# Sampled rows of V by two indirect DMAs of GpSimd a tile, in place of six register-addressed DMAs of the sync engine

## The chip, the cores and the metric

The kernel runs on one core of one Trainium2 chip. A core has a matrix engine (TensorE, here PE, with its weight loads as PEld), a vector engine (VectorE, DVE), a scalar engine (ScalarE, ACT), a general engine (GpSimd, POOL) and a sync engine (SyncE, SP), which here only issues DMAs. Each engine works through its own instructions in order and waits on semaphores of the others. Sixteen DMA engines move the data. The metric is the device time of one execution in microseconds (us).

## The reference

Block-sparse attention over 4 batches, 8 heads, 768 positions of 64 values, and then a two-layer feed-forward network (FFN) over the 3072 tokens of 512 values. A query block of 32 positions sees its own block and both neighbours, the first and the last block, and three sampled blocks; the first and the last query block see everything.

```python
scores = scale * np.matmul(q, k.transpose(0, 1, 3, 2))
mask = np.abs(blk_i - blk_j) <= 1
mask = mask | (blk_i == 0) | (blk_j == 0) | (blk_i == n_blocks - 1) | (blk_j == n_blocks - 1)
for qb in range(n_blocks):
    for kb in sampled_blocks[qb]:
        mask[qb * 32:(qb + 1) * 32, kb * 32:(kb + 1) * 32] = True
attn = softmax(np.where(mask, scores, -1e9))
x = np.matmul(attn, v)                  # heads side by side: 3072 x 512
h = x @ w_in                            # 512 -> 2048
return np.maximum(0.01 * h, h) @ w_out  # 2048 -> 512
```

`sampled_blocks` is an input (24 x 3 block numbers), so the rows that a tile needs are known only on the chip.

## The kernel before

**Tiles.** A tile `T` is two query blocks (64 queries). Each batch has 12; tile 0 holds the first and the last block and sees all keys, the other 11 see 384 gathered keys: 12 slots of 32. In 4 batches that makes 44 gathered tiles. Before the change slots 0 to 3 are the window of four consecutive blocks, 4 and 5 the first and the last block, 6 to 11 the six sampled blocks (`sampled_of`, L569). Every value is split into a high and a low half in float16, so products are done in several matmuls.

**A tile's keys and values.** `gather_k` (L576) builds `kg`, the gathered K: a copy of the window on DVE (L582), the end blocks once a batch (L585), and then for each sampled block a register load of its offset on POOL (L590, from `offs`) and a copy on POOL (L591). `gather_v` (L605) builds `vg`, the gathered V: 128 partitions by 3 chunks, slot `s` in partitions 32·(s mod 4) of chunk s // 4. V's split rows lie in a DRAM scratch tensor `scr`, 2 KB a row. SP issues one DMA for the window (L611), two for the end blocks when the buffer is first used in a batch (L616), and for each of the six sampled blocks it loads the offset into a register (L619) and issues a DMA of 32 rows (L621). `kg` and `vg` have two buffers each, so a gather for tile T waits until PE is done with tile T-2.

**The rest of a tile.** Scores `s` on PE (L651, the first factor is the transposed q, `qs`, and its copy with swapped halves, `qxs`); row maxima with the mask on DVE (L658, `mx`); exponentials on ACT (L669); normalized high halves `pp` on ACT (L687) and low halves on DVE (L691); a DMA transpose of `pp` into `pt` issued by SP (L696); the product with `vg` on PE (L722, `av`). The output goes through ACT, DVE and POOL into `x` (L729 to L740). Q is prepared in halves of an item (four tiles): scaled, transposed by a DMA on SP (L535, `qs`) and copied with swapped halves (L537, L538). K is transposed once a batch in the same way (L512, `kt`).

**The FFN.** An item's 256 tokens go through in 8 chunks: first product `h` on PE (L757), leaky maximum on ACT and DVE (L764, L768, `ht`, one buffer), the high half of `g` on DVE (L773), the low half on POOL (L774), second product `o` on PE (L787, which needs both halves). The weights arrive as 64-bit values and are decoded on DVE and ACT (L310 to L316) and split (L371 to L376) during the first 200 us or so.

**What sets the order.** The program is written as one long list of steps, by tile and head pair, with the side work in between. A scheduler with a modelled timeline then sets each engine's order, so a step whose engine changes can move others on every engine. `in_order` (L558) adds order-only dependencies that keep the register-addressed instructions of one kind in sequence.

## Time and profile before

| | us |
|---|---|
| median of 3 runs | 904.76 |
| lowest and highest | 899.24, 905.93 |
| the profiled execution | 903.64 |
| its span, first to last instruction | 902.0 |
| DMA packets of SP's queue, share of 16 engines' span | 69.4% |
| mean granted clock of TensorE | 0.941 |

The profile is of one execution. A line such as `L691 DVE ...` gives the line of the program, the engine and the operation; the name ahead of the arrow is the tile that is written, the names behind it are read. Busy time counts an engine's own instructions, not what it issues: SP's register loads and DMA issues appear only in views of its queue (`SPq`). A wait is put down to the instruction that released the waiting one last. The granted clock is the share of full speed that the throttle gave TensorE. The busy digits of PE and DVE in 40 slices of 22.6 us show two stages: DVE-heavy at first, then PE-heavy.

```profile
PE   1324536688996988998997999889998999999998
...
DVE  4988889989876857757657656658676677655221
...
PEclk9999555899997999999998999999999999999999
```

### The profile page before, as it was taken

To read this page: it belongs to the slowest core of one execution; us is meant where nothing else is said; L and a number is where in the kernel's file an instruction comes from. 1 tells how busy PE (TensorE), PEld (TensorE's weight loads), DVE (VectorE), ACT (ScalarE), POOL (GpSimd) and SP (SyncE) were. 2 spreads that over 40 slices of the span, in tenths; PEclk is the share of its full clock that TensorE was granted. 3 is DMA by queue.
4 is the path that set the end of the run, shared out by engine and by line. 5 is a ranking of instruction groups with operands and counts; after the bars stand their busy time and mean duration, and the time that the engine had idled before them with its cause. 6 is when DMAs were issued, how large, how long until landed. Compare 5 with 4: busy or idle time off the path is not lost. (4 is left out here: it accounts for less than half of the span.)

```text
span 902.0 us, 21419 instructions
## 1 busy us (share of the span) xinstructions
PE 741.3 (82%) x7020; PEld 485.8 (54%) x7020; DVE 619.6 (69%) x1643; ACT 487.2 (54%) x1063; POOL 329.2 (37%) x469
## 2 busy tenths in 40 slices
PE   1324536688996988998997999889998999999998
PEld 0213234346564655665654665556665666656674
DVE  4988889989876857757657656658676677655221
ACT  4665765658554655556546545556455556544211
POOL 0143653724124334343423443334314354431221
PEclk9999555899997999999998999999999999999999
DMA  9994687778787697675776978766676857455100
GB/s 219 274 302 114 164 236 182 196 158 160 157 186 166 143 182 158 154 153 122 177 184 142 192 140 162 162 135 150 153 143 157 146 127 164 111 127 126 10 22 24
DMA packets 333294, 139.35 MB, mean 154 GB/s; under 512 B 296061, under 2 KB 308350, under 8 KB 333182
## 3 DMA queue, kind: packets, MB, share of 16 engines
q1 hardware_dynamic: 333182, 137.98, 69.4%
q8 instruction: 55, 0.90, 0.4%
q14 instruction: 57, 0.47, 0.2%
HBM read 65.57 MB, written 12.58 MB: 87 GB/s over the span
## 5 line engine op out<-in xcount | busy, mean ns | idle before, releaser
L757 PE MATMUL h<-x,W 128*128 128x256 f16 x2304 | 279.7, 278 | 1.1 <-DVE q_tot L140 0.8
L787 PE MATMUL o<-W,g 128*128 128x512 f16 x1152 | 275.1, 384 | 5.7 <-DVE g L773 3.3
L757 PEld LDWEIGHTS <-W 128*128 128x128 f16 x2304 | 226.2, 101 | 47.9 <-issue 8.3
L774 POOL TENSOR_TENSOR g<-ht,g 128x512 f16<-128x512 f32 x96 | 113.7, 1185 | 247.8 <-DVE g L773 173.7
L591 POOL COPY kg<-kt 128x256 f16 x264 | 124.0, 488 | 179.1 <-PE s L651 100.9
L669 ACT ACTIVATE p<-p,mx 128x384 f32<-128x384 f32 x208 | 126.2, 608 | 113.1 <-DVE mx L658 83.3
L691 DVE SCALAR_TENSOR_TENSOR pp<-p,r,pp 128x384 f16<-128x384 f32 x208 | 142.0, 713 | 56.5 <-ACT pp L687 55.9
L787 PEld LDWEIGHTS <-g 128*128 128x128 f16 x1152 | 107.9, 99 | 132.3 <-issue 16.7
L687 ACT ACTIVATE pp<-p,r 128x384 f16<-128x384 f32 x208 | 115.5, 607 | 63.6 <-DMA pt<-pp 23.7
L658 DVE CUSTOM_DVE_ANT_0 p<-s,em,nsc 128x384 f32<-128x384 f32 x176 | 102.4, 610 | 29.5 <-PE s L651 29.5
L768 DVE SCALAR_TENSOR_TENSOR ht<-h,gd,ht 128x512 f32<-128x512 f32 x80 | 59.7, 747 | 63.0 <-ACT ht L764 62.8
L722 PE MATMUL av<-pt,vg 128*64 128x128 f16 x2112 | 81.7, 228 | 19.3 <-DMA pt<-pp 12.2
L722 PEld LDWEIGHTS <-vg 128*64 128x64 f16 x2112 | 71.1, 114 | 42.0 <-issue 37.1
L764 ACT ACTIVATE ht<-h,gs 128x512 f32<-128x512 f32 x80 | 54.2, 677 | 68.1 <-PE h L757 53.8
L651 PE MATMUL s<-kg,qs_q 128*64 128x384 f16 x352 | 64.7, 365 | 31.5 <-DVE mx L658 24.8
L651 PEld LDWEIGHTS <-qs_q 128*64 128x64 f16 x416 | 27.6, 114 | 99.8 <-issue 64.7
L740 POOL TENSOR_TENSOR x<-xf,x 128x256 f16<-128x256 f32 x48 | 36.8, 766 | 101.9 <-ACT x L738 101.5
L651 PE MATMUL s<-kg,qxs_q 128*64 128x384 f16 x352 | 62.9, 356 | 9.7 <-DMA qxs_q<-qs_q 9.7
L677 DVE TENSOR_SCALAR sum<-sum 128x2 f32<-128x2 f32 x96 | 32.4, 337 | 37.4 <-ACT p L669 36.9
L773 DVE CAST g<-ht 128x512 f16<-128x512 f32 x96 | 42.0, 437 | 9.4 <-PE o L787 7.8
L651 PE MATMUL s<-kt,qs_q 128*64 128x384 f16 x64 | 12.8, 394 | 33.1 <-DVE mx L658 17.1
L669 ACT ACTIVATION_READ_ACCUMULATOR p<-p,mx 128x1 f32 x208 | 39.3, 189 | 0.0
(126 smaller groups left out, 728.9 us busy)
## 6 DMA issues: line engine op xcount, KB each, us to landing
vg<-scr SPq DMA_DIRECT2D x280, 64.0 KB, 1.8
vg<-scr SPq DMA_DIRECT2D x44, 256.0 KB, 3.7
v<-in_v_dram SPq DMA_DIRECT2D x32, 192.0 KB, 5.1
qxs_q<-qs_q SPq DMA_DIRECT2D x48, 128.0 KB, 2.6
scr<-v SPq DMA_DIRECT2D x16, 384.0 KB, 5.1
W<-in_moe_w_in_dram SPq DMA_DIRECT2D x5, 1024.0 KB, 6.1
rq<-in_q_dram SPq DMA_DIRECT2D x20, 256.0 KB, 3.7
out_dram<-ob SPq DMA_DIRECT2D x20, 256.0 KB, 2.8
```

Of the source, the lines that this page charges most:

```text
L591: nc.gpsimd.tensor_copy(out=kg[:, :, slot * BLOCK:(slot + 1) * BLOCK], in_=kt[:, :, bass.ds(off, BLOCK)])
L651: nc.tensor.matmul(o, a, k, start=(n == 0), stop=(n == 1)))
L658: nc.vector.tensor_tensor_reduce(out=u.p[i], in0=u.sp[i], in1=kgs[u.b, u.T][1] if u.T else zero.to_broadcast([P, KEYS]), scale=u.nsc, scal ...
L669: nc.scalar.activation(u.p[i], u.p[i], AF.Exp, scale=-1.0, bias=u.mx[:, :1], accum_out=u.pair.sum[:, u.pi, i:i + 1])
L687: nc.scalar.activation(pp[:, 0, :], p, AF.Copy, scale=u.r)
L691: nc.vector.scalar_tensor_tensor(out=pp[:, 1, :], in0=p, scalar=u.r, in1=pp[:, 0, :], op0=ALU.mult, op1=ALU.subtract)
L722: nc.tensor.matmul(o, a, m, start=(c == 0 and l == 0), stop=(c == n - 1 and l == 1)))
L757: nc.tensor.matmul(c.ph[:, i], w, x, start=(d == 0 and m == 0), stop=(d == NP - 1 and m == 2)))
L764: nc.scalar.activation(c.t, c.ph, AF.Copy, scale=scale[1])
L768: nc.vector.scalar_tensor_tensor(out=c.t, in0=c.ph, scalar=scale[0], in1=c.t, op0=ALU.mult, op1=ALU.max)
L774: nc.gpsimd.tensor_tensor(out=c.g[:, 1], in0=c.t, in1=c.g[:, 0], op=ALU.subtract)
L787: nc.tensor.matmul(o, a, w, start=(c.first and i == 0 and m == 0), stop=(c.last and i == 1 and m == 2)))
```

## The change

The six sampled blocks of a tile are no longer fetched by SP. A table `rows` (128 partitions x 2 chunks x 11 tiles) holds, for each partition, the row of V that belongs there: block number times 32 plus the lane within the block. It is filled once, at the start: six DMAs bring each sampled block number to 32 partitions, POOL writes the partition numbers into `lane`, and DVE combines them. `gather_v` then issues two indirect DMAs on POOL's queue, each with one column of `rows` as its list of row numbers: one for chunk 1 (128 rows) and one for chunk 2 (64 rows). For that the sampled blocks must fill whole chunks from their start, so the slots are reordered: the window keeps 0 to 3, the sampled blocks take 4 to 9, the end blocks 10 and 11. The mask, the copies into `kg` and the places in `vg` follow.

```diff
     def load_constants():
...
+        nc.vector.memset(rows, 0)
+        for s_ in range(2 * NR):
+            a, r = s_ // NR, s_ % NR
+            nc.sync.dma_start(
+                out=rows[s_ % 4 * BLOCK:(s_ % 4 + 1) * BLOCK, s_ // 4, :],
+                in_=sampled.bitcast(I32)[1 + a:NB - 2 + a:2, 2 * r].unsqueeze(0).to_broadcast([BLOCK, NT - 1]))
     def build_masks():
...
+        nc.gpsimd.iota(lane, pattern=[[0, 1]], base=0, channel_multiplier=1)
+        nc.vector.tensor_scalar(out=lane, in0=lane, scalar1=BLOCK - 1, scalar2=None, op0=ALU.bitwise_and)
+        flat_rows = rows.rearrange("p c t -> p (c t)")
+        nc.vector.scalar_tensor_tensor(
+            out=flat_rows, in0=flat_rows, scalar=5, in1=lane.to_broadcast([P, 2 * (NT - 1)]),
+            op0=ALU.logical_shift_left, op1=ALU.bitwise_or)
...
-            out=mask[:, :, 6:], in0=pm.rearrange("p t a r -> p t (a r)"), scalar1=-1.0, scalar2=-NEG,
+            out=mask[:, :, 4:10], in0=pm.rearrange("p t a r -> p t (a r)"), scalar1=-1.0, scalar2=-NEG,
             op0=ALU.add, op1=ALU.mult)
-        nc.vector.memset(mask[:, :, :6], 0.0)
+        nc.vector.memset(mask[:, :, :4], 0.0)
+        nc.vector.memset(mask[:, :, 10:], 0.0)
...
-        return [(6 + a * NR + r, (2 * T - 1 + a) * NR + r) for a in range(2) for r in range(NR)]
+        return [(4 + a * NR + r, (2 * T - 1 + a) * NR + r) for a in range(2) for r in range(NR)]
...
         nc.sync.dma_start(out=vg[:, 0, :], in_=scr[b][t0:t0 + P, :])
         if vends.get(n) != b:
             vends[n] = b
-            for slot, a in ((4, 0), (5, S - BLOCK)):
-                ps, c = place(slot)
-                nc.sync.dma_start(out=vg[ps, c, :], in_=scr[b][a:a + BLOCK, :])
-        for slot, i in sampled_of(T):
-            begin = len(nc.cur_bb.bb.instructions)
-            off = nc.sync.value_load(offs[:1, i:i + 1], min_val=0, max_val=S - BLOCK)
-            ps, c = place(slot)
-            nc.sync.dma_start(out=vg[ps, c, :], in_=scr[b][bass.ds(off, BLOCK), :])
-            in_order("v", begin)
+            for i, at in enumerate((0, S - BLOCK)):
+                nc.sync.dma_start(
+                    out=vg[Q2 + i * BLOCK:Q2 + (i + 1) * BLOCK, 2, :], in_=scr[b][at:at + BLOCK, :])
+        for c, n_ in ((1, P), (2, Q2)):
+            nc.gpsimd.indirect_dma_start(
+                out=vg[:n_, c, :], out_offset=None, in_=scr[b][:, :],
+                in_offset=bass.IndirectOffsetOnAxis(ap=rows[:n_, c - 1, T - 1:T], axis=0))
```

The scheduler's order follows. Line numbers of the changed kernel are 9 to 15 higher than before (L632 is the indirect DMA, L535 becomes L550, L696 becomes L708, L774 becomes L786). First SP, in the last item of the last batch, where the second half of Q is transposed (`qs_q3_2_1`). Before:

```order
L619 TENSOR_LOAD offs_89
L619 ISA x2
L621 ISA
L621 DMA vg1_96<-scr_3_12237 32x1024
L619 TENSOR_LOAD offs_89
L619 ISA x2
L621 ISA
L621 DMA vg1_96<-scr_3_12237 32x1024
L535 DMA_TRANSPOSE qs_q3_2_1_15871<-qa_q3_2_1_15455 128x8x128
L696 DMA_TRANSPOSE pt_3_2_0_3_15928<-pp_3_2_0_2_15743 128x12x128
L537 DMA qxs_q3_2_1_15873<-qs_q3_2_1_15871 64x1024
```

SP at the same place in the changed kernel:

```order
L708 DMA_TRANSPOSE pt_3_2_0_1_13376<-pp_3_2_0_0_13268 128x12x128
L708 DMA_TRANSPOSE pt_3_2_0_3_13505<-pp_3_2_0_2_13378 128x12x128
L625 DMA vg1_98<-scr_3_10394 128x1024
L708 DMA_TRANSPOSE pt_3_2_1_1_13607<-pp_3_2_1_0_13507 128x12x128
L550 DMA_TRANSPOSE qs_q3_2_1_13448<-qa_q3_2_1_13148 128x8x128
L552 DMA qxs_q3_2_1_13450<-qs_q3_2_1_13448 64x1024
```

The sampled gathers ahead of the transposes are gone; the transpose of q moved behind a transpose of the next tile's probabilities, which it used to precede. Second POOL, in batch 1, at the low halves `g_1_1_4` and `g_1_1_6` of two FFN chunks. Before:

```order
L596 CAST em_2_2_9181<-mask_90 128x384
L774 TENSOR_TENSOR g_1_1_4_8259<-ht_1_1_4_8256,g_1_1_4_8259 128x512
L590 TENSOR_LOAD offs_89
L590 ISA x2
L590 TENSOR_LOAD offs_89
L590 ISA x2
L740 TENSOR_TENSOR x_1_2_8169<-xf_1_2_1_2_8440,x_1_2_8169 128x4x64
L774 TENSOR_TENSOR g_1_1_6_8403<-ht_1_1_6_8400,g_1_1_6_8403 128x512
```

POOL at the same place in the changed kernel:

```order
L611 CAST em_2_2_7802<-mask_92 128x384
L786 TENSOR_TENSOR g_1_1_4_7054<-ht_1_1_4_7051,g_1_1_4_7054 128x512
L632 DMA vg1_98<-scr_1_3411,rows_90 128x1024
L605 TENSOR_LOAD offs_89
L605 ISA x2
L632 DMA vg1_98<-scr_1_3411,rows_90 64x1024
L605 TENSOR_LOAD offs_89
L605 ISA x2
L752 TENSOR_TENSOR x_1_2_6964<-xf_1_2_1_2_7177,x_1_2_6964 128x4x64
L786 TENSOR_TENSOR g_1_1_6_7140<-ht_1_1_6_7137,g_1_1_6_7140 128x512
```

A pair of indirect DMAs now stands between two low halves of g. Of the 44 pairs, 6 stand directly ahead of such an instruction and 8 with one instruction between. Third DVE, at the start, where the mask is made from the block numbers. Before:

```order
L532 SCALAR_TENSOR_TENSOR qa_q0_0_0_134<-rq_0_0_0_99,q0_0_0_s_143,qa_q0_0_0_134 128x8x64
L218 TENSOR_SCALAR offs_89<-tmps_88 1x72
L222 CAST sf_168<-tmps_88 24x3
L227 TENSOR_SCALAR tmps_88<-iota_87,sf_168 24x24 x3
L228 TENSOR_TENSOR hit_171<-tmps_88,allow_86 24x24
L311 TENSOR_SCALAR W_91<-W_91 128x1024
```

DVE at the same place in the changed kernel:

```order
L547 SCALAR_TENSOR_TENSOR qa_q0_0_0_143<-rq_0_0_0_101,q0_0_0_s_152,qa_q0_0_0_143 128x8x64
L226 TENSOR_SCALAR offs_89<-tmps_88 1x72
L236 CAST sf_180<-tmps_88 24x3
L232 SCALAR_TENSOR_TENSOR rows_90<-rows_90,lane_91 128x22
L241 TENSOR_SCALAR tmps_88<-iota_87,sf_180 24x24 x3
L242 TENSOR_TENSOR hit_183<-tmps_88,allow_86 24x24
```

The instruction that completes `rows` now stands between the cast to `sf` and the first comparison, ahead of the first decoding of the weights (L311 before).

More of the change, by code (lines that the diff above doesn't have):

```diff
@@ L207, in tile_block_sparse_attention_ffn @@
     offs = cst.tile([1, NB * NR], I32, name="offs")
+    rows = cst.tile([P, 2, NT - 1], I32, name="rows")
+    lane = cst.tile([P, 1], I32, name="lane")
     mask = cst.tile([P, NT - 1, SLOTS], F32, name="mask")
@@ L252, in build_masks @@
             nc.vector.memset(mask[b, :, 0:1], NEG)
-            nc.vector.memset(mask[a, 0:1, 4:5], NEG)
-            nc.vector.memset(mask[b, NT - 2:NT - 1, 5:6], NEG)
+            nc.vector.memset(mask[a, 0:1, 10:11], NEG)
+            nc.vector.memset(mask[b, NT - 2:NT - 1, 11:12], NEG)
     WI = 512
@@ L585, in gather_k @@
             nc.vector.tensor_copy(
-                out=kg[:, :, P:P + Q2].rearrange("p h (n l) -> p h n l", l=BLOCK),
+                out=kg[:, :, KEYS - Q2:].rearrange("p h (n l) -> p h n l", l=BLOCK),
                 in_=kt.rearrange("p h (n l) -> p h n l", l=BLOCK)[:, :, 0:NB:NB - 1, :])
@@ L609, in gather_v @@
         t0 = (T - 1) * Q2
-        place = lambda slot: (slice(slot % 4 * BLOCK, (slot % 4 + 1) * BLOCK), slot // 4)
         nc.sync.dma_start(out=vg[:, 0, :], in_=scr[b][t0:t0 + P, :])
```

## The prediction

> **What bounds the kernel now.** I read the header of the page first, then the busy time of each engine in four stretches, then the waits of TensorE (PE) in the two long ones.
>
> ```profile
> span 902.0 us, 21419 instructions
> PE 741.3 (82%) x7020; PEld 485.8 (54%) x7020; DVE 619.6 (69%) x1643; ACT 487.2 (54%) x1063; POOL 329.2 (37%) x469
> ...
> 0.00:67.50 67.50, 16.33 (x86) 10.44 (x86) 48.65 (x144) 38.57 (x68) 14.03 (x21) 1.00 1.12 265
> 67.50:225.00 157.50, 95.58 (x997) 65.40 (x998) 141.57 (x351) 101.68 (x203) 72.86 (x88) 0.78 0.74 173
> 225.00:860.00 635.00, 591.28 (x5686) 385.24 (x5684) 419.92 (x1134) 340.70 (x785) 233.10 (x352) 0.97 0.69 147
> 860.00:902.00 42.00, 38.08 (x256) 24.71 (x253) 9.42 (x16) 6.21 (x10) 9.25 (x8) 0.99 0.04 13
> ```
>
> The columns of the stretches are PE, weight loads, DVE, ACT, POOL, then the granted clock, the share of the DMA engines and GB/s. From 225 to 860 us PE is busy 591.3 of 635 us: it is the bound, and only 43.7 us of idle time can be won there. From 67.5 to 225 us DVE is busy 141.6 of 157.5 us (it decodes the weights beside the attention), so DVE is the bound there and at most 15.9 us can be won. The last 42 us are FFN matmuls that the change does not touch. SP has no busy time in such a table; what it is worth shows only in who waits for its DMAs. First PE's waits from 67.5 to 225 us, then from 225 to 860 us (total, times, longest):
>
> ```profile
> PE av L722 <- DMA pt<-pp: 12.7, 6, 4.7
> ...
> PE s L651 <- DMA qxs_q<-qs_q: 3.7, 2, 2.8
> PE s L651 <- DMA qs_q<-qa_q: 3.2, 1, 3.2
> ```
>
> ```profile
> PE s L651 <- DVE mx L658: 12.5, 6, 3.8
> PE av L722 <- DMA pt<-pp: 7.2, 4, 3.9
> PE s L651 <- DMA kt<-k_k: 6.9, 1, 6.9
> PE s L651 <- DMA qxs_q<-qs_q: 6.0, 4, 2.4
> ...
> PE s L651 <- DMA qs_q<-qa_q: 3.3, 2, 2.2
> ```
>
> All three DMAs named (pt, qs, qxs) are issued by SP, in order, between the blocks of V's gather. In neither list does PE wait for vg itself by a visible amount: the gathered rows arrive early enough today.
>
> **Part 1: what leaves SP.** One sampled block costs SP these instructions (min/median/max in ns):
>
> ```profile
> L619 SPq TENSOR_LOAD <-offs x264: 262/276/1097, 25.4 to 828.8; - x132
> L619 SPq FUSED_REGOPS  x264: 152/155/187, 25.9 to 829.1; - x132
> ...
> L621 SPq FUSED_REGOPS  x264: 37/37/52, 67.8 to 829.4; - x132
> L621 SPq MOVE vg<-scr x264: 29/29/38, 67.9 to 829.5; - x132
> L621 SPq DMA_DIRECT2D vg<-scr x264: 315/317/1605, 68.0 to 829.6; - x132
> ```
>
> 276 + 155 + 37 + 29 + 317 = 814 ns, times 264 blocks: 215 us of SP's time goes, about 4.9 us a tile. Almost all of it lies beside PE's work. Where it does not, it looks like this (SP's rows, then PE's):
>
> ```profile
> 789.12 6.28 SPq L621 DMA_DIRECT2D vg<-scr  x6
> 795.51 1.27 SPq L535 DMA_TRANSPOSE qs_q<-qa_q  x1
> ...
> 798.93 0.73 PE L651 MATMUL s<-kg,qs_q 128*64 128x384 f16 x4 [2.16 <-DMA qs_q<-qa_q]
> ```
>
> Six gathers hold SP for 6.28 us, the transpose of q goes out behind them, and PE stands 2.16 us. So what can come back from 225 us on is pt 7.2 + qxs 6.0 + qs 3.3 = 16.5 us; the 6.9 us for kt is one wait at a change of batch that hangs on the preparation of K, and I leave it out. The other end is 0: a transpose also has a landing time of its own, and in the new order the transposes are placed anew (in the rows of SP that the change section shows, qs now stands behind a pt that waits for the softmax). Half of the waits is as near to one end as to the other, and the one gap that I followed was caused by the gather, so I take **-8 us**, bounds -16.5 and 0. From 67.5 to 225 us PE waits 12.7 + 3.7 + 3.2 = 19.6 us for the same DMAs, but DVE is the bound and its whole idle time is 15.9 us; a PE that starts earlier helps only where DVE then waits less. I take a quarter of the 15.9, **-4 us**, bounds -15.9 and 0. What is late next where such a wait goes: the PSUM banks that DVE must empty (mx, 12.5 us).
>
> The plain load of a tile's window (L611) and the two end blocks stay on SP; SP's waits for a free vg stay with them. The order of the slots changes only which columns of kg, the mask and vg are written: same shapes, so 0. One small mask memset becomes two, at the very start, where DVE idles until the first sums of K: 0.
>
> **Part 2: the new index table at the start.** Six DMAs of 32 x 11 single words fill `rows`, in SP's queue ahead of the first transposes of K and q, and a DVE instruction that needs all six stands in DVE's order right behind the cast to sf. SP's and DVE's rows there, and what the DMA queues did from 5 to 30 us:
>
> ```profile
> 11.16 0.36 SPq L215 DMA_DIRECT2D tmps<-in_sampled_blocks_dram  x1
> 11.64 1.59 SPq L512 DMA_TRANSPOSE kt<-W  x1
> ...
> 15.73 0.16 DVE L222 CAST sf<-tmps 24x3 f32<-24x3 int32 x1 [0.51 <-DMA tmps<-in_sampled_blocks_dram]
> 15.93 0.51 DVE L227 TENSOR_SCALAR tmps<-iota,sf 24x24 f32<-24x24 f32 x3
> ...
> DMA packets 16061, 6.58 MB, mean 263 GB/s; under 512 B 15317, under 2 KB 15318, under 8 KB 16060
> ...
> q1 hardware_dynamic: 16060, 6.58, 119.7%
> ```
>
> Issuing: 6 x 0.36 = 2.2 us. Moving: 6 x 352 = 2112 packets of 4 bytes; a packet there took 1.197 x 16 x 25 us / 16060 = 29.8 ns of one engine, so 2112 x 29.8 ns / 16 = 3.9 us. Together 6.1 us by which kt, qs and DVE's instruction come later. DVE waits at 15.73 us already and is busy almost without a break after 22 us, so most of the delay runs through the DVE-bound stage; some is swallowed by the waits of the first 30 us. I take **+4 us**, bounds 0 and +6.1; a gain is excluded, since only a wait is added. The iota on POOL and the small `lane` instruction stand ahead of DVE's first sums, which wait for the loads of K: 0, hidden by these.
>
> **Part 3: what comes to POOL.** 88 indirect DMAs, two a tile, 128 and 64 rows. No row of before shows one. The nearest rows are POOL's own instructions that write 128 partitions:
>
> ```profile
> L774 POOL TENSOR_TENSOR g<-ht,g 128x512 f16<-128x512 f32 x96 | 113.7, 1185 | 247.8 <-DVE g L773 173.7 <-DVE sum L677 34.2 <-DVE r L678 9.5
> L591 POOL COPY kg<-kt 128x256 f16 x264 | 124.0, 488 | 179.1 <-PE s L651 100.9 <-issue 36.4 <-DMA kt<-W 18.1
> ...
> L374 POOL TENSOR_TENSOR W<-W 128x1024 f16<-128x1024 f32 x12 | 28.6, 2391 | 2.9 <-ACT W L373 2.2 <-POOL kg L591 0.5 <-ACT x L738 0.3
> ```
>
> Bounds 0.49 and 2.39 us each; I take 1.185 us, the middle row, for want of one that is nearer: 88 x 1.185 = 104 us more on POOL, from 329 to 433 of 902. POOL is no bound, but it works in order, and the low half of g (L774) that PE's second FFN product needs is in that order. How much room g has (POOL's rows, then PE's):
>
> ```profile
> 445.76 1.37 POOL L774 TENSOR_TENSOR g<-ht,g 128x512 f16<-128x512 f32 x1 [5.34 <-DVE g L773]
> ...
> 453.31 1.16 POOL L774 TENSOR_TENSOR g<-ht,g 128x512 f16<-128x512 f32 x1 [0.62 <-DVE sum L677]
> ...
> 458.30 1.16 POOL L774 TENSOR_TENSOR g<-ht,g 128x512 f16<-128x512 f32 x1 [1.36 <-DVE g L773]
> ...
> 447.19 1.90 PE L787 MATMUL o<-W,g 128*128 128x512 f16 x8 [0.22 <-POOL g L774]
> ...
> 458.23 1.89 PE L787 MATMUL o<-W,g 128*128 128x512 f16 x8
> ...
> 461.81 2.76 PE L787 MATMUL o<-W,g 128*128 128x512 f16 x12
> ```
>
> The three g end at 447.13, 454.47 and 459.46 us and are used at 447.19, 458.23 and 461.81: room of 0, 3.8 and 2.4 us, about 2.0 in the mean. In the new order of POOL 6 of the 44 pairs stand right ahead of a g and 8 more with one instruction between. A pair of 2.4 us is then 0.4 us longer than the room: 14 x 0.4 = **+5 us**. At 0.49 us it fits (0); at 2.39 us it is 14 x (4.8 - 2.0) = +39 us. A gain is excluded, POOL only gets work. The copies of kg have a tile's time of room and cost 0 while that holds. The DMA also waits on POOL, for PE to be done with the vg buffer two tiles before (SP did that until now), and behind it wait g, x and kg. I price that wait at 0 because in POOL's new order the pair mostly stands behind a g or x that itself waits for later work than that PE product.
>
> The Trainium skill, page "DMA: Bandwidth & Descriptors", section "Latency and other measured facts", puts the emission on GpSimd's cores at about 1 us; by it a pair is about 2.0 us, an estimate that just fits the room and makes this term 0 and the sum about 5 us lower. No run here has shown such a DMA yet.
>
> **The sum.** The profiled execution took 903.6 us, 1.6 of it around the span; the median of the runs shown is 904.8 (899.2 to 905.9), so I add 1.1. 903.6 - 8 - 4 + 4 + 5 = 900.6, and with the 1.1 about **902 us**: no change that a measurement tells (about 1%, 9 us, is what one can tell).
>
> **Rivals.** *SP's waits all go (faster).* For it: the gap at 798.93 us, and that such blocks, 4.9 us a tile, stand in all 44 tiles. Against: PE finds other work for most of that time already. It gives the full -16.5, half of DVE's idle time (-8), +4 for the table, POOL hidden: 904.8 - 20.5 = **884 us**.
>
> *POOL delays g (slower).* One mechanism: a pair ahead of g in POOL's order takes longer than g's room. It decides from about 1.6 us a DMA on, where 14 x (3.2 - 2.0) = 17 us: 904.8 - 12 + 4 + 17 = 914. At 1.8 us it is 14 x 1.6 = 22, less 12, plus 4: 904.8 + 14 = **919 us**; at 2.39 us 936 us. For it: the room of 0 at 447.19, and that ACT already waits for POOL:
>
> ```profile
>   ACT ht L764: 15.5, 8
> ...
>   PE o L787: 0.6, 2
> ```
>
> These are waits for POOL's g (total, times). Against: PE's own share of them is 0.6 us, and POOL is idle for 63% of the span.
>
> *Copies of DVE hold POOL's DMAs up (slower).* DVE casts g 96 times:
>
> ```profile
> L773 DVE CAST g<-ht 128x512 f16<-128x512 f32 x96 | 42.0, 437 | 9.4 <-PE o L787 7.8
> ```
>
> If each DMA waited for one such cast, a pair would be 0.87 us longer: 14 x (0.4 + 0.87) = 18 instead of 5, and the time 902 + 13 = **915 us**. Against: these casts are busy for under 5% of the span. The Trainium skill, page "SBUF — State Buffer", section "SBUF: two separate sides", warns of just this: while DVE runs such a copy GpSimd cannot write its DMA descriptors, and it advises the sync queue instead. The trace can bear on it only through POOL's copies of kg, whose mean of 488 ns leaves little room for such holds.
>
> *The transfer was hidden anyway.* Nothing on either queue matters and only the table counts: 904.8 + 4 = 909 us, within 1%.
>
> **Chances.** Forecast and hidden transfer, both within 1%: 0.42. SP's waits go: 0.30, all of it faster. POOL delays g: 0.22; held by DVE: 0.06; both slower. So faster 0.30, within 1% 0.42, slower 0.28. Range: below, all gains at their ends and no cost give 904.8 - 16.5 - 15.9 = 872; I cut at 882, which holds the first rival's 884. Above, 936 is the far end; 924 holds 919 and leaves about a tenth out on either side. The forecast's own range is 896 to 909.
>
> **What would show it.** Right: SP's rows without L619, vg rows on POOL of 1.0 to 1.5 us each; PE's waits for pt, qs and qxs after 225 us at about 8 us instead of 16.5; PE's wait for POOL's g up by some 5 us; DVE's first mask instruction (before at 15.93 us) some 6 us later; the 67.5 to 225 us stage ending about where it did. Wrong: DMA rows on POOL of over 1.6 us; a new wait of PE for vg, which I priced at 0; waits of POOL for PE ahead of its DMAs with g behind them; or a granted clock in the second stretch that is far from 0.78, which would move the time for a reason that I do not price.

## The result and the profile after

| | before | after |
|---|---|---|
| median of 4 runs, us | 904.42 | 917.0 |
| lowest and highest, us | 899.24, 905.93 | 915.16, 918.1 |
| profiled execution and its span, us | 903.64, 902.0 | 916.05, 914.1 |
| mean granted clock of TensorE | 0.941 | 0.936 |

The changed kernel is slower: ratio 1.0145, 95% interval 1.0111 to 1.0179, which is 13 us. Below, the gain or loss of a kernel is its ratio less one, times 904.4 us.

The stretches of the changed kernel (us, then the busy time of PE, weight loads, DVE, ACT and POOL, the granted clock, the share of the DMA engines, GB/s):

```profile
0.00:67.50 67.50, 15.43 (x76) 9.11 (x76) 41.76 (x139) 35.54 (x61) 12.87 (x22) 1.00 0.94 237
67.50:225.00 157.50, 98.70 (x988) 68.78 (x990) 147.99 (x348) 100.76 (x204) 92.33 (x106) 0.74 0.83 189
225.00:860.00 635.00, 589.83 (x5598) 381.46 (x5599) 437.21 (x1143) 339.64 (x785) 302.35 (x420) 0.97 0.73 145
860.00:914.00 54.00, 49.43 (x364) 31.91 (x362) 10.28 (x18) 9.05 (x14) 11.06 (x10) 0.98 0.06 20
```

From 225 to 860 us PE is no less idle than before (589.8 us of work against 591.3), although SP has lost six DMAs and six register loads a tile. Over the whole span PE is idle just as long as before, 160.7 us (902.0 less 741.3 us of work, 914.1 less 753.4). By the profile, then, the 12 us that the span has grown are longer times of the same 7020 matmuls (their ends are partly modelled). The granted clock is lower from 67.5 to 225 us, 0.74 against 0.78, which is one of the signs that the prediction named; but it is 0.75 there in `registers_fixed_rows` below too, which takes as long as the kernel before. POOL has 302 us instead of 233. DVE's timeline at the start shows what the table does:

```profile
14.99 0.15 DVE L236 CAST sf<-tmps 24x3 f32<-24x3 int32 x1 [0.65 <-DMA tmps<-in_sampled_blocks_dram]
22.48 0.18 DVE L232 SCALAR_TENSOR_TENSOR rows<-rows,lane 128x22 int32<-128x22 int32 x1 [7.33 <-DMA rows<-in_sampled_blocks_dram]
22.58 0.51 DVE L241 TENSOR_SCALAR tmps<-iota,sf 24x24 f32<-24x24 f32 x3
```

DVE stands 7.33 us for the six DMAs of single words; its first mask instruction starts at 22.58 us instead of 15.93. The indirect DMAs on POOL, and what POOL waited for ahead of them (us, times):

```profile
L632 POOL DMA_INDIRECT vg<-scr,rows x88: 899/998/1801, 68.5 to 836.9; - x88
its engine sat idle before it (us, times) until:
  PE av L734: 74.8, 23
```

An issue takes 1.0 us in the median. But ahead of 23 of them POOL stands, 74.8 us in all, until PE is done with vg, and everything behind it in POOL's order stands with it. PE's waits from 225 to 860 us for the transposes that SP issues have not fallen:

```profile
PE av L734 <- DMA pt<-pp: 10.1, 7, 4.3
PE s L663 <- DMA qxs_q<-qs_q: 9.3, 6, 4.5
...
PE s L663 <- DMA qs_q<-qa_q: 2.9, 3, 2.0
```

That is 22.3 us; it was 16.5. What stands ahead of these transposes shows in SP's own waits, which the prediction did not look at. First those of the kernel before, then those of the changed one (total, times, longest):

```profile
SPq L816 <- ACT ob L805: 66.0, 6, 40.4
SPq L696 <- PE av L722: 14.7, 11, 1.7
...
SPq L696 <- DVE pp L691: 9.5, 3, 8.0
SPq L611 <- PE av L722: 7.7, 6, 2.0
```

```profile
SPq L708 <- DVE pp L703: 96.9, 38, 10.6
SPq L625 <- PE av L734: 82.0, 25, 7.9
```

The 66.0 us for `ob` are stores of the output, 64.1 of them after 825 us. While attention ran, SP waited little before: the waits that its view lists from 225 to 825 us add up to 110 us, against 380 in the changed kernel. It reached the window's load (L611) so late that the buffer was nearly always free already. Now it waits, and in its new order a transpose of probabilities stands 38 times until DVE has written pp, with qs, qxs and the loads queued behind.

### The profile page after: what moved, and what is told of

It reads as the page before. It is cut to its first block, busy times and chain, and to the rows that moved or that the text cites. A ratio compares the mean times of both kernels' runs of the same rounds, so it can differ in the third digit from the quotient of the medians.

```text
span 914.1 us, 19932 instructions
## 1 busy us (share of the span) xinstructions
PE 753.4 (82%) x7020; PEld 491.3 (54%) x7020; DVE 637.2 (70%) x1647; ACT 485.0 (53%) x1063; POOL 418.6 (46%) x558
## 5 line engine op out<-in xcount | busy, mean ns | idle before, releaser
L799 PE MATMUL o<-W,g 128*128 128x512 f16 x1152 | 278.9, 386 | 9.9 <-DVE g L785 5.5
L786 POOL TENSOR_TENSOR g<-ht,g 128x512 f16<-128x512 f32 x96 | 115.8, 1206 | 206.3 <-DVE g L785 158.7
L703 DVE SCALAR_TENSOR_TENSOR pp<-p,r,pp 128x384 f16<-128x384 f32 x208 | 154.4, 772 | 32.4 <-ACT pp L699 31.4
L632 POOL DMA_INDIRECT vg<-scr,rows x88 | 94.0, 1068 | 94.3 <-PE av L734 74.8
L734 PE MATMUL av<-pt,vg 128*64 128x128 f16 x2112 | 87.6, 234 | 25.4 <-DMA pt<-pp 17.8
L734 PEld LDWEIGHTS <-vg 128*64 128x64 f16 x2112 | 74.2, 119 | 51.3 <-issue 47.0
L785 DVE CAST g<-ht 128x512 f16<-128x512 f32 x96 | 44.3, 462 | 11.6 <-PE o L799 10.1
L689 DVE TENSOR_SCALAR sum<-sum 128x2 f32<-128x2 f32 x96 | 27.7, 288 | 23.1 <-ACT p L681 22.3
L538 ACT ACTIVATE qa_q<-rq 128x512 f16<-128x512 f32 x25 | 15.7, 627 | 48.7 <-DMA rq<-in_q_dram 48.7
```

The source lines that it names most:

```text
L632: nc.gpsimd.indirect_dma_start(out=vg[:n_, c, :], out_offset=None, in_=scr[b][:, :], in_offset=bass.IndirectOffsetOnAxis(ap=rows[:n_, c - ...
L703: nc.vector.scalar_tensor_tensor(out=pp[:, 1, :], in0=p, scalar=u.r, in1=pp[:, 0, :], op0=ALU.mult, op1=ALU.subtract)
L734: nc.tensor.matmul(o, a, m, start=(c == 0 and l == 0), stop=(c == n - 1 and l == 1)))
L786: nc.gpsimd.tensor_tensor(out=c.g[:, 1], in0=c.t, in1=c.g[:, 0], op=ALU.subtract)
L799: nc.tensor.matmul(o, a, w, start=(c.first and i == 0 and m == 0), stop=(c.last and i == 1 and m == 2)))
```

## The experiments

### The table at the start

Theory A: the delay of the start runs through to the end. Theory B: the loss is POOL's. Kernel `table_only` adds the table (`load_constants` and `build_masks` as in the change) to the kernel before, used by nobody:

```diff
+    rows = cst.tile([P, 2, NT - 1], I32, name="rows")
+    lane = cst.tile([P, 1], I32, name="lane")
```

> The kernel before with the row table of the change added at the start (six DMAs of single words, the lane numbers, the combining DVE instruction) and used by nobody; V's rows still come by SP's register-addressed DMAs, and every engine keeps the order of before. Theory A (the table delays the start, and the delay runs through to the end): DVE stands 7.33 us at the combining instruction in the changed kernel, so about 904.4 + 7 = 911 us, ratio 1.007. Theory B (the loss is POOL's: its waits for PE and its 94 us of DMA issues): the start is swallowed, 904 to 906 us.

Measured: 910.15 us, ratio 1.0062 (1.0033 to 1.009), +5.6 us. `table_whole_words` is the changed kernel with other words in the table:

```diff
-                in_=sampled.bitcast(I32)[1 + a:NB - 2 + a:2, 2 * r].unsqueeze(0).to_broadcast([BLOCK, NT - 1]))
+                in_=sampled.bitcast(I32).rearrange("(o a) b -> o (a b)", o=1)[:, 6 * s_:6 * s_ + NT - 1].to_broadcast([BLOCK, NT - 1]))
```

> The changed kernel with the same six DMAs of the table, each of which reads 11 neighbouring words instead of 11 words that lie 48 bytes apart: 192 packets instead of 2112, the order of every engine but for this unchanged. The row numbers in the table are then others (still rows of V), so the sampled rows of V are not the reference's. Theory A: the wait of 7.33 us falls to 2 or 3 us and the time by 4 to 5, from 917 to about 912 us; DVE's first mask instruction 4 to 5 us earlier than 22.6. Theory B: no change, 917.

Measured: 910.52 us, ratio 1.0087 (1.0054 to 1.0119). DVE's wait fell as expected:

```profile
17.72 0.18 DVE L232 SCALAR_TENSOR_TENSOR rows<-rows,lane 128x22 int32<-128x22 int32 x1 [2.15 <-DMA rows<-in_sampled_blocks_dram]
```

5.2 us less of wait (the instruction starts 4.8 us earlier), 5.2 us less of time. So theory A holds for 5 to 6 of the 13 us. `table_from_row` keeps the table and drops its DMAs:

```diff
-    row = tmps[:1, 6:6 + 2 * NB * NR].bitcast(I32)
+    row = tmps[:, 6:6 + 2 * NB * NR].bitcast(I32)
...
+            nc.vector.scalar_tensor_tensor(
+                out=rows[ps, s_ // 4, :],
+                in0=row[ps, :].rearrange("p (n r l) -> p n r l", r=NR, l=2)[:, 1 + a:NB - 2 + a:2, r, 0],
+                scalar=5, in1=lane[ps, :].to_broadcast([BLOCK, NT - 1]),
+                op0=ALU.logical_shift_left, op1=ALU.bitwise_or)
```

> The changed kernel with the table built without DMAs of its own: the one DMA that brings the block numbers to partition 0 now brings them to all 128 partitions (576 bytes each), and six small DVE instructions shift, add the lane and place them. Everything is computed. The scheduler's order differs somewhat from the changed kernel's. Theory A: the whole 7 us of the start come back, less six DVE instructions of about 0.1 us: 917 - 6.5 = 910 to 911 us, ratio 1.007. Theory B: 917, ratio 1.014. If the rest of the loss comes from the new order rather than from POOL, the time may miss both by a few us.

Measured: 917.39 us, ratio 1.0177 (1.0134 to 1.022): a miss. In the first 67.5 us PE does 17.52 us of work instead of 15.43, so the start came back, and it was lost again from 225 us on, in an order of the scheduler that differs from the changed kernel's. A different order can thus be worth some 8 us by itself (1.0177 here against 1.0087 for `table_whole_words`, whose table costs no less); where it mattered, I chose edits that keep the order.

### What SP's gather had cost

`plain_on_sp` has neither table nor POOL's DMAs:

```diff
-            nc.gpsimd.indirect_dma_start(
-                out=vg[:n_, c, :], out_offset=None, in_=scr[b][:, :],
-                in_offset=bass.IndirectOffsetOnAxis(ap=rows[:n_, c - 1, T - 1:T], axis=0))
+            nc.sync.dma_start(out=vg[:n_, c, :], in_=scr[b][c * P:c * P + n_, :])
```

> The slots of the change, but the two DMAs of a tile (128 and 64 rows) are plain DMAs on SP that read fixed rows of V, with no table and no DMA on POOL: the sampled rows of V are not the reference's. It shows what freeing SP of the register loads and four of six DMAs is worth by itself. My forecast's relief of 12 us: 892 us, ratio 0.987. If the relief is worth nothing and POOL is what costs (theory B): 904. If SP's relief is worth nothing and the new order itself costs what theory A leaves open (917 - 7 - 904 = 5 to 6 us): 910.

Measured: 855.27 us, ratio 0.9473 (0.9441 to 0.9506). None of the three: freeing SP is worth 48 us, four times my forecast. The scheduler gave every engine a new order for it, so this is the relief together with that order. PE's waits from 225 to 860 us are then:

```profile
PE s L647 <- DMA qxs_q<-qs_q: 8.7, 6, 2.5
PE s L647 <- DVE mx L654: 5.5, 6, 1.6
...
PE k_sum L126 <- ACT k_k L495: 0.4, 1, 0.4
```

The waits for pt, qs and kt are no longer listed, those for mx have fallen from 12.5 us, and those for `k_k` from 5.0, where the kernel before had this line:

```profile
PE k_sum L126 <- ACT k_k L494: 5.0, 4, 2.3
```

`six_plain_on_sp` has six DMAs of 32 rows again, without register loads:

```diff
-            off = nc.sync.value_load(offs[:1, i:i + 1], min_val=0, max_val=S - BLOCK)
...
-            nc.sync.dma_start(out=vg[ps, c, :], in_=scr[b][bass.ds(off, BLOCK), :])
+            nc.sync.dma_start(out=vg[ps, c, :], in_=scr[b][slot * BLOCK:(slot + 1) * BLOCK, :])
```

> The kernel before in slots and engines, with six DMAs of 32 rows a tile on SP, but at fixed rows and so without the register loads (0.50 us of SP each of a block's 0.81): the sampled rows of V are not the reference's. If the register loads are what SP's gather costs the kernel before: close to plain_on_sp, 855 to 865 us. If it is the number of DMAs: 885 to 904 us.

Measured: 853.61 us, ratio 0.9439 (0.9401 to 0.9476). The number of DMAs costs nothing that shows (the order of every engine differs here too). Its SP waits for a free vg ahead of the window's load, as a queue with time to spare does, and from 225 us on PE gets its full clock:

```profile
SPq L611 <- PE av L719: 74.7, 20, 5.5
```

```profile
225.00:860.00 635.00, 606.65 (x5872) 400.40 (x5870) 425.40 (x1137) 345.91 (x790) 241.98 (x359) 1.00 0.70 145
```

`loads_fixed_rows` puts the loads back and does not use them; `registers_fixed_rows` also uses them, with fixed numbers in the registers. Both keep the order of PE, ACT and POOL of the kernel before. The second against the kernel before:

```diff
+        nc.gpsimd.iota(offv, pattern=[[BLOCK, 2 * NR]], base=P, channel_multiplier=0)
...
-            off = nc.sync.value_load(offs[:1, i:i + 1], min_val=0, max_val=S - BLOCK)
+            off = nc.sync.value_load(offv[:1, slot - 6:slot - 5], min_val=0, max_val=S - BLOCK)
```

> six_plain_on_sp (853.6 us) with the register loads put back on SP, one ahead of each of the six DMAs, but the DMAs still read fixed rows and do not use the registers, so the sampled rows of V are not the reference's. The order of PE, ACT and POOL is exactly that of the kernel before. If what the kernel before pays is SP's time for the loads (its queue is issuing for nearly all of the time from 225 to 825 us): about as before, 898 to 906 us. If it pays for the scattered rows or the register addressing of the DMAs: 853 to 865 us.

> The kernel before with every instruction and the order of every engine kept (one small iota on POOL added at the start), only that SP loads its six registers from a table of six fixed offsets: each tile then fetches the same 192 rows of its batch, which are not the reference's sampled rows. loads_fixed_rows, where the DMAs did not use the registers, took 881 us, the kernel before 903. If the 22 us between them are the register addressing of the DMAs: 903 us. If they are the scattered rows: 881 us.

Measured: 881.09 us, ratio 0.9752 (0.9727 to 0.9776), and 902.26 us, ratio 0.9989 (0.9963 to 1.0016). So the scattered rows cost nothing, and the register addressing 21 us, with the order kept. The loads cost 28 us against `six_plain_on_sp`, where the order of every engine differs as well, so these 28 are loads and order together. A load takes 276 + 155 ns of SP. The addressing takes only 37 + 29 ns, and the DMA itself 317 instead of 306 ns:

```profile
L621 SPq DMA_DIRECT2D vg<-scr x264: 302/306/1664, 67.9 to 808.2; - x132
```

264 x 431 ns = 114 us of SP cost 28 us, and the last 264 x 77 ns = 20 us cost 21. I read this as a queue that is full: the first work put on it is hidden, the last is paid one for one. That is not shown, and full cannot mean that SP never stands: its listed waits from 225 to 825 us add up to 139 us in `loads_fixed_rows` and 110 us in the kernel before (276 in `six_plain_on_sp`). `less_on_sp` moves V's loads, K's from the second batch on and the stores of the output to ACT, and was to test the reading from another side:

```diff
-            nc.sync.dma_start(out=t[:, :, h, :], in_=v[b, 2 * hp + h].rearrange("(c p) d -> p c d", p=P))
+            nc.scalar.dma_start(out=t[:, :, h, :], in_=v[b, 2 * hp + h].rearrange("(c p) d -> p c d", p=P))
...
-                nc.sync.dma_start(out=out[r0:r0 + P, :], in_=ob)
+                nc.scalar.dma_start(out=out[r0:r0 + P, :], in_=ob)
```

> The kernel before, with its register-addressed gathers left as they are, and other work taken off SP: the loads of V, of K from the second batch on and the stores of the output are issued by ACT. That is about 37 us of the some 576 us for which SP's queue is busy from 225 to 825 us. Everything is computed. If SP's queue is a bound of the kernel before: a gain of a quarter of the 50 us that freeing it of 131 us of loads brought, 888 to 896 us. If not: 902 to 908 us, or slower by what ACT gets.

Measured: 908.64 us, ratio 1.0063 (1.0036 to 1.0089): a miss, and no clean one. The start came later (in the first 225 us PE did 101.6 us of work, before 111.9); from 225 to 860 us it did 4 us more than before (595.4 against 591.3). It neither shows nor refutes the full queue.

### What POOL's DMAs cost

Theory C: POOL's wait for PE, with kg, g and x behind it. Theory D: the issues themselves. Theory E: the scheduler's order. `plain_on_pool` against `plain_on_sp`:

```diff
-            nc.sync.dma_start(out=vg[:n_, c, :], in_=scr[b][c * P:c * P + n_, :])
+            nc.gpsimd.dma_start(out=vg[:n_, c, :], in_=scr[b][c * P:c * P + n_, :])
```

> plain_on_sp (855.3 us) with its two plain DMAs a tile issued from POOL instead of SP; again fixed rows of V, so the sampled rows are not the reference's, and no table. Theory C: POOL again waits for PE at the gather: 905 to 912 us, as the changed kernel without its table. Theory D: the same 905 to 912, but with little waiting of POOL for PE. If it is the list of row numbers (the indirection) that costs, and not the engine: 855 to 865 us.

Measured: 905.02 us, ratio 1.0011 (0.9988 to 1.0033). The list of rows is not it: 49 us go when the same two plain DMAs move from SP to POOL. POOL waits 55.8 us for PE there, and an issue takes 0.56 us. That is as theory C had it, at the lower end of its range. `behind_x` is `table_from_row` with the gather written behind x, and its two DMAs ordered behind it:

```diff
+        for i in nc.cur_bb.bb.instructions[begin:] if x else []:
+            tc.add_manual_dep(i, x, mybir.DependencyInfo(
+                mybir.DependencyClass.NoSync, mybir.DependencyReason.DATA), reason="behind x")
...
-                vfree[0] += pr.T > 0
```

> The kernel of table_from_row (917.4 us), with one order set: the two indirect DMAs of a tile stand on POOL behind the subtraction that writes x of two tiles before, which by itself waits until PE is done with that tile's vg. Everything is computed. Theory C (what costs is POOL's wait for PE at the gather, 74.8 us in the changed kernel, with kg, g and x queued behind it): that wait goes to nearly 0 and the time comes close to plain_on_sp, 860 to 875 us. Theory D (POOL's 94 us of issuing, and what it does to DVE): no change, 910 to 917 us. Theory E (the scheduler's order of the whole program): a time that follows from neither, with the wait gone and the time still above 890.

Measured: 895.53 us, ratio 0.9898 (0.9861 to 0.9934), 25 us less than `table_from_row`. POOL's wait for PE's product is gone from the list of these DMAs:

```profile
L632 POOL DMA_INDIRECT vg<-scr,rows x88: 899/990/1705, 61.8 to 820.3; - x88
its engine sat idle before it (us, times) until:
  issue: 15.6, 54
```

The time is above the 860 to 875 us of theory C, and a wait gone with the time still above 890 us is what theory E said. The edit brought 25 us, but the order of every engine changed with it, and POOL's waiting in good part moved. First `table_from_row`, then `behind_x` (total, times, longest):

```profile
POOL kg L604 <- PE s L661: 73.1, 24, 8.3
POOL vg L630 <- PE av L732: 56.3, 21, 9.9
POOL x L750 <- ACT x L748: 31.3, 18, 4.0
```

```profile
POOL kg L604 <- PE s L666: 96.1, 28, 8.6
POOL x L755 <- ACT x L753: 81.6, 30, 9.3
```

Nor do PE and ACT wait clearly less for POOL in sum: ACT for g 27.3 us and then 24.4, PE for g 3.1 and then none listed, PE for kg 6.0 and then 11.0. So the 25 us are what this place of the DMAs is worth; how much of it is POOL's wait and how much the order is not shown. 38 us over `plain_on_sp` were left. `pool_beside` adds to `plain_on_sp`, in `gather_v`:

```diff
+            nc.gpsimd.indirect_dma_start(
+                out=spare[:n_, c - 1, :], out_offset=None, in_=scr[b].rearrange("s (a c) -> (s a) c", c=16),
+                in_offset=bass.IndirectOffsetOnAxis(ap=lane[:n_, :1], axis=0))
```

> plain_on_sp (855.3 us) and beside it on POOL, for each tile, two indirect DMAs of 128 and 64 rows of 32 bytes into a small tile that nobody reads, so POOL has the issues of the changed kernel and no wait for vg. The sampled rows of V are still the fixed ones. Theory C: 855 to 862 us, since there is no wait. Theory D: the issues alone cost, 890 to 912 us, with DVE's pp (728 ns in plain_on_sp, 772 in the changed kernel) slow again.

Measured: 896.96 us, ratio 0.9942 (0.9917 to 0.9968). It does not tell what I wanted: nothing held the idle DMAs back, so they came in bunches (17 of them between 459 and 491 us), and POOL waited 37.7 us for loads, stores and earlier idle DMAs ahead of them. `pool_dma_spaced` sets the same two DMAs behind each x in `tile_evac`, ordered as in `behind_x`, and `pool_work_spaced` puts additions there instead:

```diff
+        for i in range(6 if pr.T else 0):
+            nc.gpsimd.tensor_tensor(out=flat_mask, in0=flat_mask, in1=zero.to_broadcast([P, (NT - 1) * SLOTS]), op=ALU.add)
```

> plain_on_sp (855.3 us) with pool_beside's idle indirect DMAs (rows of 32 bytes that nobody reads) set behind each tile's x instead of wherever the scheduler likes: in pool_beside nothing held them back, and they stood in POOL's order in bunches of many pairs. The sampled rows of V are the fixed ones. Theory D (each issue costs): 885 to 900 us, as pool_beside. If it was the bunches that cost: 855 to 866 us.

> plain_on_sp (855.3 us) with six additions of zero to the mask on POOL behind each tile's x (about 0.37 us each, 98 us in all), in place of DMAs. The sampled rows of V are the fixed ones. If POOL's mere occupation costs, as pool_dma_spaced within 8 us. If it is something about DMAs on POOL's queue: near 855 us while pool_dma_spaced is slower.

Measured: 873.36 us, ratio 0.9665 (0.9639 to 0.9691), and 863.69 us, ratio 0.9559 (0.9532 to 0.9587). Spaced issues cost 17 us over `plain_on_sp`, and POOL's plain occupation, in smaller pieces (0.41 us each), 8. Both expectations of the first miss: bunches were more than half of what `pool_beside` lost, not all. The second lies between its two. `one_list_two_rows` halves the issues:

```diff
+        nc.gpsimd.indirect_dma_start(
+            out=vg[:96, 1:3, :].rearrange("p c x -> p (c x)"), out_offset=None,
+            in_=scr[b].rearrange("(n l) x -> n (l x)", l=2),
+            in_offset=bass.IndirectOffsetOnAxis(ap=rows[:96, T - 1:T], axis=0))
```

> behind_x (895.5 us) with one indirect DMA a tile instead of two: each of 96 row numbers names two neighbouring rows of V (4 KB), which go to chunks 1 and 2 of one partition, and the end blocks, kg and the mask follow that layout (the mask copy becomes two). Everything is computed. If POOL's issues are what is left of the loss (theory D: 855 to 895 us for 88 DMAs, whose time is nearly the same for 128 rows, 0.98 us, and 64 rows, 0.90), half of them should bring back about half: 872 to 882 us, ratio 0.97. If the loss is in the rows moved by POOL's queue, or in the order: 890 to 900 us.

Measured: 887.08 us, ratio 0.982 (0.9786 to 0.9855), 7 us less than `behind_x` by the ratios and between the two ranges. That is about half of 17, not half of 38.

### What was left: 21 us between `behind_x` and `pool_dma_spaced`

Three candidates: the later place of the gather in the program, the scattered rows, SP's order. `plain_late` has `plain_on_sp`'s DMAs written where `behind_x` has them; `list_fixed_rows` reads the partition numbers in place of a column of `rows`, with the order of `behind_x` kept:

```diff
+        vfree[0] += pr.T > 0
...
-                vfree[0] += pr.T > 0
```

```diff
-                in_offset=bass.IndirectOffsetOnAxis(ap=rows[:n_, c - 1, T - 1:T], axis=0))
+                in_offset=bass.IndirectOffsetOnAxis(ap=lane[:n_, :1], axis=0))
```

> plain_on_sp (855.3 us) with the gather written into the program where behind_x has it, once the x of two tiles before is done; still two plain DMAs on SP at fixed rows (not the reference's sampled rows). behind_x is 22 us above pool_dma_spaced. If that rest comes from the later place of the gather: 870 to 880 us. If it comes from the rows' way through POOL's queue and its in-order work: 853 to 860 us.

> behind_x (895.5 us) with the order of every engine kept, only that each indirect DMA reads a list of fixed rows (the partition numbers) instead of a column of the table: always the same rows of the batch, not the reference's sampled rows. If the 22 us between pool_dma_spaced and behind_x are the scattered rows: 873 to 878 us. If they are the way of 17 MB of rows through POOL's queue: 892 to 897 us.

Measured: 856.76 us, ratio 0.9469 (0.944 to 0.9499), and 899.1 us, ratio 0.996 (0.9937 to 0.9984). Neither the place nor the scattered rows. `mixed` is `behind_x` with one of the two DMAs on POOL and two blocks on SP:

```diff
+        for slot, i in sampled_of(T)[4:]:
...
+            off = nc.sync.value_load(offs[:1, i:i + 1], min_val=0, max_val=S - BLOCK)
...
+            nc.sync.dma_start(out=vg[ps, c, :], in_=scr[b][bass.ds(off, BLOCK), :])
...
-        for c, n_ in ((1, P), (2, Q2)):
+        for c, n_ in ((1, P),):
```

> behind_x with chunk 1 (four blocks) by one indirect DMA of POOL and chunk 2 (two blocks) by SP's register-addressed DMAs as before the change, with the table from the row of block numbers. Everything is computed. If the two costs add by their counts: 855 + half of POOL's 40 us + a third of SP's 50 us = 890 to 893 us. If a cost only sets in once a queue is full: SP with a third of its loads is not, and the time is that of one_list_two_rows or less, 870 to 887 us.

Measured: 870.8 us, ratio 0.9644 (0.9619 to 0.9668): faster than both kernels, with everything computed, and below the 890 that costs added by counts would give. Unlike before the change, its SP waits for a free vg, as a queue with time to spare does, and it is held by pp less than in `behind_x` (34.8 us against 92.5):

```profile
SPq L624 <- PE av L743: 81.3, 23, 6.6
...
SPq L717 <- DVE pp L712: 34.8, 17, 6.9
```

`idle_loads` leaves all rows to POOL and gives SP two register loads a tile that nobody uses:

```diff
+        for slot, i in sampled_of(T)[4:]:
+            begin = len(nc.cur_bb.bb.instructions)
+            nc.sync.value_load(offs[:1, i:i + 1], min_val=0, max_val=S - BLOCK)
+            in_order("v", begin)
```

> behind_x (895.5 us) with two register loads a tile put back on SP whose registers nobody uses; all rows still come by POOL's two indirect DMAs, and everything is computed. In behind_x and the changed kernel SP stands 93 and 97 us at transposes of the probabilities (pt) that wait for DVE's pp, with other DMAs queued behind them; in mixed (870.8 us), which has such loads and half of POOL's DMAs, 35 us. If SP's order, with the transposes placed too early, is what is left of the loss: SP's wait for pp falls well below 93 us and the time towards mixed, 870 to 885 us. If it is POOL's second DMA a tile with its rows: 893 to 900 us.

Measured: 878.21 us, ratio 0.9719 (0.9677 to 0.9762): 16 us faster than `behind_x` for added work. SP's wait for pp fell from 92.5 us (`behind_x`) to 66.0, and PE's wait for pt from 225 to 860 us from 9.8 us to below what is listed, while that for qxs rose from 7.3 to 10.6 (the profile of `idle_loads` is of its longest execution, 885.06 us):

```profile
SPq L711 <- DVE pp L706: 92.5, 39, 8.1
```

```profile
SPq L715 <- DVE pp L710: 66.0, 31, 5.4
```

So 16 of the 21 us are the order that the scheduler makes once SP's load is light, and not the rows that POOL moves; the other 5 stay open. That it is SP's transposes rather than another engine's new order fits these rows but is not shown: the loads moved the order of every engine.

## Why the prediction was wrong

The forecast was 902 us, the result 917. By the runs, with 904.4 for before, the changed kernel is made up so:

| part | forecast, us | measured, us | by |
|---|---|---|---|
| SP freed | -12 | -48 | `plain_on_sp` |
| table at the start | +4 | +5 to +6 | `table_only`, `table_whole_words` |
| POOL's issues | +5 | +17 | `pool_dma_spaced` |
| POOL's wait for vg, with the order that goes with it | 0 | +25 | `behind_x` against `table_from_row` |
| order | 0 | +16 | `idle_loads` against `behind_x` |

The last column of numbers adds to 15 or 16, the change cost 13. The kernels of a pair differ in order too, so a single entry is good to some 8 us, not better. That the sum comes so near is partly luck: it leaves out the 5 us that stayed open, and `table_from_row`, which has no delay from the table, is 3 us slower than the changed kernel and not 5 faster. Free of this splitting are the two ends: -48 us to `plain_on_sp`, and from there +61 us to the changed kernel (0.0672 x 904.4).

**Part 1, SP's relief, was too small and its bounds too narrow.** The failed step is that SP's worth was read only from PE's waits for SP's DMAs ("what can come back ... 16.5 us"). By these names the forecast was even met: in `plain_on_sp` they are 8.7 us, 7.8 less than before, and I had said 8. But PE's idle time after 225 us fell by 26.9 us (from 47.6 to 20.7), the rest of it mainly under the names mx, kt and `k_k`, which I had left out. That a late transpose delays DVE and ACT, and so brings these waits about, fits this and is not shown by itself.

Second, in the first 225 us PE did 125.7 us of work instead of 111.9. DVE's idle time from 67.5 to 225 us, my cap for that stage, fell only from 15.9 to 12.4 us while PE's work there rose from 95.6 to 108.2, so it was no cap. Third, the 43.7 us of idle time were no upper end, because PE's busy time shrinks as well, for the same 7020 matmuls: 741.3 us before, 733.4 in `plain_on_sp`, 728.7 in `six_plain_on_sp`. The three make up the whole: 26.9 + 13.8 + 7.9 = 48.6 us, the difference of the spans, 902.0 and 853.4.

The granted clock goes with the third: from 225 to 860 us it is 0.97 before and 1.00 in `six_plain_on_sp`. In the kernel before, around the wait of 6.91 us for kt (which ends at 281.32 us):

```profile
275.00:277.50 2.50, 0.00 (x0) 0.00 (x0) 0.72 (x3) 0.00 (x0) 0.00 (x0) 0.87 0.62 119
277.50:280.00 2.50, 0.00 (x0) 0.00 (x0) 0.00 (x0) 0.00 (x0) 0.00 (x0) 0.50 1.03 229
280.00:282.50 2.50, 1.18 (x8) 0.72 (x10) 1.20 (x3) 1.11 (x3) 0.96 (x2) 0.50 1.06 211
282.50:285.00 2.50, 2.50 (x31) 1.97 (x28) 2.50 (x11) 1.41 (x5) 1.79 (x4) 0.50 0.83 170
285.00:287.50 2.50, 2.50 (x16) 1.82 (x15) 1.58 (x5) 1.73 (x4) 1.90 (x4) 0.58 0.38 88
287.50:290.00 2.50, 2.50 (x22) 1.86 (x20) 2.13 (x6) 2.10 (x7) 1.78 (x5) 1.00 0.37 83
```

After the wait PE works at half its clock until about 287 us, nearly 6 us more, so this wait cost some 3 us above its own length. Behind the gap of 2.16 us that the prediction followed it is the same: in the four microseconds from 799 us the granted clock is 0.55, 0.50, 0.50 and 0.75. The Trainium skill, page "TensorE: Matmul & The Clock Gate", section "Part 1: The HAM clock gate (the "warmup" mystery)", says that the gate falls to half rate after an idle window of about 3.4 us and opens again after a busy one. The rows agree in kind; but the clock fell here some 2.4 us after PE's last work, sooner than a whole such window (0.87 in the stretch to 277.5 us, the wait having begun at 274.41).

**Part 2, the table, was right in mechanism and size:** DVE's first mask instruction came 6.65 us later (forecast some 6), the time 5 to 6 us (forecast 4, bounds 0 and 6.1).

**Part 3, POOL.** The price of an issue was right: 1.07 us in the mean, forecast 1.185. The Trainium skill, page "DMA: Bandwidth & Descriptors", section "Latency and other measured facts", gives about 1 us for the emission. The trace agrees with it for these DMAs; the plain ones of `plain_on_pool` took 0.56 us. That a pair of 2 us then just fits the room and costs nothing, the runs do not bear out. The sum over 14 pairs ahead of a g was too small, 17 us instead of 5; spaced additions of no DMA cost 8 of these already, by occupation alone. Nor did it come by way of g: PE's wait for POOL's g was to rise by some 5 us, but it went from 0.6 us to none listed, and ACT's from 15.5 to 22.3. The other failed step is the wait for vg, priced at 0 "because in POOL's new order the pair mostly stands behind a g or x that itself waits for later work than that PE product". It does not: 23 of the DMAs waited, up to 9.8 us, 74.8 us in all. I had looked at the order and inferred a time from it. Setting the DMAs behind x brought 25 us, with the reservation on the order that stands above; a new wait of PE for vg is not listed. The prediction did name this wait, with g behind it, among what would make it wrong.

**The order itself** was given no price beyond the remark that transposes are placed anew. It showed in PE's waits for pt, qxs and qs (22.3 us, forecast 8).

**Rivals.** "SP's waits all go" was right about SP and still too small; POOL took it back. "POOL delays g" came out near its time, not by its condition: it was to decide from 1.6 us a DMA. "Copies of DVE hold POOL's DMAs up": the median of 998 ns leaves no room for holds of 437 ns on most of them. The traces show something the other way round, which the prediction put at nothing: DVE's own `pp` instructions (208 of them) take 728 ns in the mean in `plain_on_sp`, 765 in `pool_dma_spaced`, 772 in the changed kernel and 784 in `behind_x`, that is 7 to 12 us more of DVE's busy time; with additions on POOL instead of DMAs it is 734. What this costs in time was not separated; it is not the last 16 us, since `idle_loads` has 785 ns. "Hidden anyway": refuted by `plain_on_sp`. Errors of some 36 us on one side and some 54 on the other made a forecast that missed by 15; that it missed by no more is luck.

## What to carry to other kernels

Read an issuing queue by its own waits: a queue that almost never waits for a free buffer is late, and freeing it is worth more than the waits that carry its name. When work moves to an engine that also computes, price what stands behind it in that engine's order by a run and not by the order alone. A DMA that waits for a buffer can be set behind an instruction that already waits for the same thing (25 us here, with the new order). Where a full queue and a busy engine can share the work, split it: half the DMAs on POOL and a third of the loads on SP took 870.8 us (with the table from the row of block numbers and the order behind x), against 904.4 with all on SP and 917 with all on POOL.

## What the runs showed that was not expected

- An indirect DMA of POOL takes nearly the same time for 128 rows (0.96 us at least, 0.99 in the median, in `mixed`, which has only these) and for 64 (0.90 at least): it is the number of DMAs that counts, not their rows.
- Sampled rows of 2 KB (in blocks of 32) cost nothing measurable against always the same rows (`registers_fixed_rows` 0.9989, and `list_fixed_rows` no faster than `behind_x`).
- Two idle register loads a tile on SP made a kernel 16 us faster, by the order that they gave it.
